# Decays moved into the mask tiles and onto the keys, GpSimd left out of the attention, and a new order of the loads

## The chip, the cores and the metric

One program on one core of a Trainium2 chip. The metric is the time of one execution in microseconds (us), median of three runs. The engines are named as in the profile: PE (TensorE; PEld is its weight load), DVE (VectorE), ACT (ScalarE), POOL (GpSimd) and SP, whose queue issues the DMAs.

## The reference

Retention attention (a causal product with a decay instead of a softmax), then two feed-forward blocks on the 2304 tokens of all batches:

```python
# q, k, v: (4 batches, 8 heads, 576 tokens, 64)
scores = scale * np.matmul(q, k.transpose(0, 1, 3, 2))
gamma = 1.0 - 2.0 ** (-5.0 - np.arange(H, dtype=np.float32))
Dmat = np.where(rel >= 0, gamma[:, None, None] ** rel[None, :, :], 0.0)   # rel = query position - key position
x = np.matmul(scores * Dmat[None, :, :, :], v)          # then to (2304, 512)
h = x @ w_in                                            # 512 -> 2048
x = (h * np.cos(h)) @ w_out
xn = x / rms * rms_g
g = xn @ w_gate                                         # 512 -> 1536
out = (silu(g) * (xn @ w_val)) @ w_out2
```

## The kernel before

The decay of a query at position i for a key at position j is gamma^i times gamma^-j. Tokens of a batch are cut into four chunks of 128 and one of 64 (`NFULL`, `REST`); a pair k is one chunk of two neighbouring batches, so there are ten pairs, 0 to 9: pairs 0 to 3 are the full chunks of batches 0 and 1, pair 4 their short one, 5 to 9 the same for batches 2 and 3.

For each chunk PE makes scores (`scores`, two PSUM banks), DVE multiplies them by the triangular mask (`masked`, two instructions), and PE multiplies the values by them (`values`). What earlier chunks add comes through a running sum of key times value (`sums_kv`), which ACT copies out of PSUM (`copy_state`) and PE multiplies by the queries (`from_state`). Before all this POOL has scaled the values by gamma^-j (`scale_values`), and behind it DVE scales the outputs by gamma^i while it takes them out of PSUM into `xall` (`result`, two instructions a pair); ACT makes the tables `gam` for that, one per chunk place (`decay`).

Weights of the first feed-forward block arrive as 64-bit words in 16 blocks w0 to w15 of 1 MiB. Each is turned into two float parts by eight steps in a chain: ACT size, DVE clamp, DVE shift, (ACT low), DVE high, DVE add, ACT cast, DVE rest. A step i of that block is a hidden product h_i (12 matmuls), the gate (ACT turns, DVE remainder, ACT sine, DVE product, ACT cast ghi, DVE low glo) and an output product out_i (12 matmuls). The first six steps (h0 to h5) take token tile 0 with w0 to w5, the next sixteen take token tile 1 with w0 to w15. Scores, masks and early hidden products share three PSUM banks (tag `g`), given out in turn.

The first 22 steps and the attention are laid out by a planner (`opening`, `lay_out`): each piece of work is a `Task` with an engine, an assumed duration and a key, and the order in which the planner picks them is the order of the instructions on each engine. The loads of the SP queue follow the list `PLAN`: a chunk's number, or -1 for the next weight block. Everything behind the opening is written out in a fixed order. The engines take their instructions strictly in that order.

Of the kernel before, what the change touches and what calls it, by code (L numbers as in the profile page):

```python
# [30 lines left out]
P = 128  # L31
# [9 lines left out]
NCH = NFULL + 1  # L41
NW1 = NF1
# [27 lines left out]
LEAD = 11.8  # L70
EARLY = 8
# [8 lines left out]
PLAN = [0, 5, 1, 6, 2, 7, -1, 3, 8, 4, 9, -1, 10, 15, 11, 16, -1, 12, 17, 13, 18, 14, 19, -1, -1, -1, -1, -1, -1, -1, -1, -1, -1, -1, -1, -1]  # L80
# [6 lines left out]
def body(ctx: ExitStack, tc, qkv, qkr, vr, w1, w2, rg, gq, gk, mask, out):  # L87
# [192 lines left out]
    first = []  # L280

    def load_tokens(part):
        for b, x in enumerate(first):
            nc.sync.dma_start(x[:, part], qkv[b, 0, :, part])

    def load(n):

        b, c = chunks[n]
        x = wa.tile([P, 4, DM], F32, tag="w", name="x")
        if n in (0, NCH):  # L290
            first.append(x)
            for src, dst in ((qkv[b, c, :, 0], x[:, 0]), (qkv[b, c, :, 1], x[:, 1]), (gk, gk_sb), (mask, mask_sb))[:2 if n else 4]:
                nc.sync.dma_start(dst, src)
        elif c < NFULL:
            nc.sync.dma_start(x, qkv[b, c])
        else:
            nc.sync.dma_start(x[:, :2, :NPAIR * REST], qkr[b])
            for a in range(2):
                nc.sync.dma_start(x[half(a), 2], vr[b])
        blocks = lambda a: a[:, :NPAIR * width(c)].rearrange("p (a i) -> p a i", a=NPAIR)  # L300
        ld[n] = blocks(x[:, 0]), blocks(x[:, 1]), x[:, 2], x[:, 3]
# [23 lines left out]
    def scores(n):  # L325
        w = width(chunks[n][1])
        kt, qt, _, _ = ld[n]
        ps = raw_scores[n] = [ps_tile().rearrange("p (h i) -> p h i", h=NPAIR) for _ in range(2)]
        for p in range(NPAIR):
            for hh in range(2):  # L330
                nc.tensor.matmul(ps[hh][keys(w, hh), p, :w], kt[half(hh), p, :], qt[half(hh), p, :], start=True, stop=True)

    def masked(n, hh):
# [4 lines left out]
                                mask_sb[r, r].unsqueeze(1).to_broadcast([w, NPAIR, w]), op=ALU.mult)  # L338

    def from_state(n):  # L340
        b, c = chunks[n]
        w, q, k = width(c), b % 2, b // 2 * NCH + c
        qt = ld[n][1]
# [22 lines left out]
    def copy_state(k):  # L366
        nc.scalar.copy(state, total[0])

    def values(n):
        b, c = chunks[n]  # L370
        w, q, k = width(c), b % 2, b // 2 * NCH + c
        vv = ld.pop(n)[2]
# [7 lines left out]
        del sc[n, 0], sc[n, 1]  # L380

    def result(k, a):
# [3 lines left out]
        nc.vector.tensor_tensor(x, outputs[k][a][..., :w], gam[c][:, a::2, :].unsqueeze(1).to_broadcast([P, 2, 2, w]), op=ALU.mult)  # L386
# [464 lines left out]
    def opening():  # L851

        lead = lambda k: 10.0 + 3.15 * k
        unit = lambda i: 31.3 + 6.8 * i if i < FIRST else 31.3 + 6.8 * FIRST + 20.0 * (i - FIRST)
# [3 lines left out]
        last_load = [None]  # L858

        def chain(x):  # L860
            last_load[0] = x
            return x

        for n in PLAN:
            if n >= 0:
                size = 0.0 if n == 0 else 1.5 if n == NCH else 2.45 if chunks[n][1] < NFULL else 0.95
                loads[n] = chain(Task("SP", size, lambda n=n: load(n), (), ones("wa"), behind=last_load[0]))
                if n == NCH:
                    parts = [chain(Task("SP", 1.25, lambda part=part: load_tokens(part), (), behind=last_load[0])) for part in (2, 3)]
                    gams = {0: chain(Task("SP", 0.6, lambda: nc.sync.dma_start(gam0, gq), (), behind=last_load[0]))}  # L870
            else:
                k = len(raws)
                raws[k] = chain(Task("SP", 2.45, lambda k=k: blocks1.append(Block(w1[k], wa if k < NSLOT_A else late["wb"])),
                                     (), ones("wa" if k < NSLOT_A else "wb"), behind=last_load[0]))
        for c in range(1, NCH):
            gams[c] = Task("ACT", 4 * 0.29, lambda c=c: decay(c), [gams[0]], key=lead(c) - 1.0)
        froms, before = {}, []
        for k in range(B // 2 * NCH):
# [5 lines left out]
            scaled = {n: Task("POOL", 1.25, lambda n=n: scale_values(n), [loads[n] if k else parts[0]], key=at) for n in pair}  # L884
# [440 lines left out]
```

## Time and profile before

| | |
|---|---|
| median of 3 runs | 890.64 us (889.91 to 890.96) |
| the profiled execution | 889.95 us |
| its span in the profile | 888.1 us (1.85 us lie around it) |
| busy share of the span | PE 97%, DVE 75%, ACT 52%, POOL 10% |
| mean granted clock of TensorE | 0.998 |

A row of the timeline gives start, duration, engine, line of the kernel, what is written from what, and in brackets how long the engine stood idle before it and what ended that. Durations of neighbouring instructions of one engine can overlap a little, so the distance from start to start is what one instruction costs.

### The profile page before, as it was taken

How to read it: one execution, taken by the hardware profiler on the slowest of the kernel's cores; microseconds unless marked ns; L12 is line 12 of the kernel's file. 1: busy time of each engine (PE TensorE's matmuls, PEld its weight loads, DVE VectorE, ACT ScalarE, POOL GpSimd, SP SyncE). 2: the span in 40 equal slices, each digit the busy share in tenths (PEclk: the TensorE clock that was granted, in tenths of full speed). 3: DMA queues.
4: the chain of work that ended last, by engine and by line, in shares of the span. 5: the costliest groups of instructions: out<-in, count | busy, mean ns of one | idle time of the engine just before them, and what ended most of it. 6: DMA issues, size and time to landing. Idle time of an engine off the chain costs nothing.

```text
span 888.1 us, 14679 instructions
## 1 busy us (share of the span) xinstructions
PE 862.8 (97%) x5738; PEld 785.9 (88%) x5738; DVE 666.3 (75%) x1004; ACT 464.2 (52%) x795; POOL 88.2 (10%) x97
## 2 busy tenths in 40 slices
PE   7797899999999999999999999999999999999998
PEld 6686688878888888998888999999999999999998
DVE  3897999947779977897874989698665598443594
ACT  3327687547565556675656755454443354333351
POOL 2340000000000000002343444100000000000000
PEclk9999999999999999999999999999999999999999
DMA  8999700124434443334786888998777798777793
GB/s 325 373 365 389 289 9 1 47 96 123 152 114 145 143 142 107 108 126 135 244 284 219 293 298 310 344 310 286 256 255 251 213 295 286 260 256 256 208 302 110
DMA packets 62085, 193.73 MB, mean 218 GB/s; under 512 B 5696, under 2 KB 23744, under 8 KB 53568
## 3 DMA queue, kind: packets, MB, share of 16 engines
q1 hardware_dynamic: 62016, 192.80, 63.7%
q8 instruction: 45, 0.74, 0.3%
q14 instruction: 24, 0.20, 0.1%
HBM read 143.49 MB, written 49.28 MB: 217 GB/s over the span
## 4 chain that ended last, share of the span: by engine, by line
PE 80%; DMA 8%; DVE 6%; ACT 2%; issue 2%; SPq 1%; POOL 1%; DVEq 0%; ACTq 0%; POOLq 0%
PE h L1077 14%; PE acc L1122 13%; PE acc L1077 13%; PE acc L242 9%; PE acc L241 9%; PE acc L243 9%; DMA raw<-w_dram 3%; PE h L242 3%; PE h L241 3%; PE h L243 3%; DMA x<-qkv_dram 3%; PE h L1122 2%; DVE w L135 2%; DMA so<-w 1%; POOL z L637 1%
## 5 line engine op out<-in xcount | busy, mean ns | idle before, releaser
L1077 PE MATMUL acc<-w 128*128 128x384 f32 x720 | 140.1, 335 | 0.5
L1077 PE MATMUL h<-w 128*128 128x384 f32 x720 | 139.0, 335 | 0.6 <-DVE SV L1059 0.6
L1077 PEld LDWEIGHTS acc<-w 128*128 128x128 f32 x720 | 125.5, 188 | 2.4 <-DVE v L1065 2.3
L1077 PEld LDWEIGHTS h<-w 128*128 128x128 f32 x720 | 125.8, 188 | 1.5 <-DVE SV L1059 1.2
L242 PE MATMUL acc<-glo,w 128*128 128x512 f32 (+1 forms) x320 | 118.0, 369 | 1.5 <-DVE glo L135 1.5
L241 PE MATMUL acc<-ghi,w 128*128 128x512 f32 (+1 forms) x320 | 118.4, 370 | 1.1 <-ACT ghi L513 1.1
L243 PE MATMUL acc<-ghi,w 128*128 128x512 f32 (+1 forms) x320 | 117.8, 368 | 0.0
L637 POOL TENSOR_TENSOR z<-z 128x256 f32<-128x256 f32 x72 | 64.6, 900 | 428.3 <-DMA z<-w 363.1
L1122 PE MATMUL acc<-w 128*128 128x256 f32 x846 | 104.1, 283 | 0.0
L1122 PEld LDWEIGHTS acc<-w 128*128 128x128 f32 x846 | 103.0, 191 | 0.2 <-DVE w L135 0.2
L241 PEld LDWEIGHTS acc<-ghi,w 128*128 128x128 f32 x320 | 60.3, 189 | 12.1 <-ACT ghi L513 1.5
L242 PEld LDWEIGHTS acc<-glo,w 128*128 128x128 f32 x320 | 60.3, 188 | 12.0 <-DVE glo L135 2.2
L243 PEld LDWEIGHTS acc<-ghi,w 128*128 128x128 f32 x320 | 60.4, 189 | 10.0
L1065 DVE TENSOR_TENSOR v<-s,acc 128x384 f32<-128x384 f32 x54 | 29.8, 551 | 52.3 <-PE acc L1077 39.5
L1105 ACT CAST w<-SV 128x768 fp32r<-128x768 f32 x55 | 42.5, 832 | 34.0 <-DVE SV L1110 18.2
L135 DVE TENSOR_TENSOR w<-SV,w 128x768 fp32r<-128x768 f32 x55 | 50.0, 953 | 13.5 <-ACT w L1105 13.5
L506 ACT ACTIVATE r<-r,half_pi 128x512 f32<-128x512 f32 (+1 forms) x80 | 54.6, 683 | 8.7 <-DVE r L503 8.5
L1043 ACT COPY s<-h 128x384 f32<-128x384 f32 x54 | 25.9, 480 | 58.9 <-PE h L1077 57.5
L241 PE MATMUL h<-xhi,w 128*128 128x512 f32 (+1 forms) x152 | 55.9, 368 | 0.0
L243 PE MATMUL h<-xhi,w 128*128 128x512 f32 (+1 forms) x152 | 55.8, 367 | 0.0
L241 PE MATMUL acc<-xhi,w 128*128 128x512 f32 (+1 forms) x152 | 55.8, 367 | 0.0
L243 PE MATMUL acc<-xhi,w 128*128 128x512 f32 (+1 forms) x152 | 55.7, 367 | 0.0
(126 smaller groups left out, 1568.1 us busy)
## 6 DMA issues: line engine op xcount, KB each, us to landing
w<-so SPq DMA_DIRECT2D x42, 768.0 KB, 6.1
w<-s SPq DMA_DIRECT2D x24, 1024.0 KB, 5.0
raw<-w_dram SPq DMA_DIRECT2D x36, 512.0 KB, 4.1
w<-s SPq DMA_DIRECT2D x24, 768.0 KB, 4.4
raw<-w_dram SPq DMA_DIRECT2D x16, 1024.0 KB, 10.8
x<-qkv_dram SPq DMA_DIRECT2D x14, 1024.0 KB, 14.5
s<-w SPq DMA_DIRECT2D x12, 1024.0 KB, 6.3
w<-t SPq DMA_DIRECT2D x36, 256.0 KB, 2.3
```

The lines of the kernel that those rows point to most:

```text
L135: eng.tensor_tensor(dst, src, hi.bitcast(F32), op=ALU.subtract)
L241: nc.tensor.matmul(dst, a[0], b[0], start=start, stop=False)
L242: nc.tensor.matmul(dst, a[0], b[1], start=False, stop=False)
L243: nc.tensor.matmul(dst, a[1], b[0], start=False, stop=stop)
L506: nc.scalar.activation(s["r"], s["r"], AF.Sin, bias=half_pi, scale=1.0)
L637: nc.gpsimd.tensor_tensor(z[:, dst], z[:, a], z[:, b], op=op)
L1043: nc.scalar.copy(t[:, :HALF], bank)
L1065: nc.vector.tensor_tensor(t, s, bank, op=ALU.add)
L1077: nc.tensor.matmul(bank, w[:, wp, kc * P:(kc + 1) * P], x[:, kc], start=k in (0, 1, 3) and kc == 0 and m == 0, stop=kc == 1 and m == 2, sk ...
L1105: nc.scalar.copy(t[:, 0], src)
L1122: nc.tensor.matmul(bank, s[:, a, i % 2, m * P:(m + 1) * P], wi[:, b], start=start and i == 0 and p == 0 and m % 2 == 0, stop=i == NPR - 1 ...
```

## The change

Values are no longer scaled and POOL does nothing in the attention. gamma^-j within a chunk goes into the mask: ACT makes three tables `falling` once, and `masked` multiplies by them. For the sums, ACT scales the keys in place by gamma^-j of the whole sequence, eight instructions for a pair (`scale_keys`), and puts the power of the chunk's place into the copy of the state, now four instructions (`copy_state`). `result` uses one table `gam` for all chunk places. A pair's operands lie in two tiles of 1 MiB (keys and queries of both chunks; values and keys by token of both chunks), the short pair's in one. `PLAN` now lists pairs: all of batches 0 and 1 come ahead of w0, pairs 5 to 7 ahead of w1, pair 8 ahead of w2, pair 9 ahead of w3.

```diff
-LEAD = 11.8
-EARLY = 8
+LEAD = 16.4
+EARLY = 7
...
-PLAN = [0, 5, 1, 6, 2, 7, -1, 3, 8, 4, 9, -1, 10, 15, 11, 16, -1, 12, 17, 13, 18, 14, 19, -1, -1, -1, -1, -1, -1, -1, -1, -1, -1, -1, -1, -1]
+PLAN = [0, 1, 2, 3, 4, -1, 5, 6, 7, -1, 8, -1, 9, -1, -1, -1, -1, -1, -1, -1, -1, -1, -1, -1, -1, -1]
...
-    def decay(c):
-        gam[c] = ap1.tile([P, NPAIR, width(c)], F32, name=f"gam{c}")
+    def fall(a):
+        r, w = (half(1), REST) if a == 2 else (slice(None), P)
         for p in range(NPAIR):
-            nc.scalar.activation(gam[c][:, p, :], gam0[:, p, :width(c)], AF.Copy, scale=later[:, c, p:p + 1])
...
-    def scale_values(n):
-        b, c = chunks[n]
-        v3 = ld[n][2].rearrange("p (h d) -> p h d", h=H)
-        nc.gpsimd.tensor_tensor(v3, v3, vg_sb[:, c, :].unsqueeze(2).to_broadcast([P, H, D]), op=ALU.mult)
+            nc.scalar.activation(falling[a][r, p, :], mask_sb[r, P - w:], AF.Copy, scale=factors[r, NCH + a, p:p + 1])
+
+    def scale_keys(k):
+        kk, c = ld[k][1][:, 2:], k % NCH
+        for h in range(H):
+            x = kk[:, :, h * D:(h + 1) * D]
+            nc.scalar.activation(x, x, AF.Copy, scale=decays[:, c * H + h:c * H + h + 1])
...
         nc.vector.tensor_tensor(s[r, :, :w], raw_scores[n][hh][r, :, :w],
-                                mask_sb[r, r].unsqueeze(1).to_broadcast([w, NPAIR, w]), op=ALU.mult)
+                                falling[hh if w == P else 2 * hh][r, :, :w], op=ALU.mult)
...
     def copy_state(k):
-        nc.scalar.copy(state, total[0])
+        for p in range(NPAIR):
+            nc.scalar.activation(state[:, :, p, :], total[0][:, :, p, :], AF.Copy, scale=factors[:, k % NCH + 1, p:p + 1])
...
-        nc.vector.tensor_tensor(x, outputs[k][a][..., :w], gam[c][:, a::2, :].unsqueeze(1).to_broadcast([P, 2, 2, w]), op=ALU.mult)
+        nc.vector.tensor_tensor(x, outputs[k][a][..., :w], gam[:, a::2, :w].unsqueeze(1).to_broadcast([P, 2, 2, w]), op=ALU.mult)
...
-        lead = lambda k: 10.0 + 3.15 * k
-        unit = lambda i: 31.3 + 6.8 * i if i < FIRST else 31.3 + 6.8 * FIRST + 20.0 * (i - FIRST)
+        lead = lambda k: 10.0 + 3.4 * k if k < 8 else 37.0 + 16.0 * (k - 8)
+        unit = lambda i: 39.0 + 12.3 * i if i < FIRST else 39.0 + 12.3 * FIRST + 5.4 * (i - FIRST)
...
+        for k in PLAN:
+            if k == 0:
+                start = [fetch(0.0, load_first, "wa"), fetch(1.3, lambda: load(0, 0, range(1, 2)))]
+                loads[0] = [start[1], fetch(2.5, lambda: load(0, 1), "wa")]
+                gams = fetch(0.7, lambda: nc.sync.dma_start(gam, gq))
+            elif k > 0:
+                loads[k] = [fetch(2.5, lambda k=k, side=side: load(k, side), "wa") for side in range(1 if k % NCH == NFULL else 2)]
...
-            scaled = {n: Task("POOL", 1.25, lambda n=n: scale_values(n), [loads[n] if k else parts[0]], key=at) for n in pair}
...
+                adding = [Task("ACT", 8 * 0.29, lambda k=k: scale_keys(k), [loads[k][1]], key=at - 1.0)]
                 for n in pair:
-                    sums = [Task("PE", 0.52, lambda n=n: sums_kv(n), [scaled[n], loads[n] if k else parts[1]] + before + sums, ones("st") if c == 0 and n == pair[0] else (),
-                                 key=at + 0.1, more=0.25, mode="columns")]
-                before = [Task("ACT", 0.55, lambda k=k: copy_state(k), sums + last + froms.get(k - 1, []), (),
+                    adding = [Task("PE", 0.52, lambda n=n: sums_kv(n), before + adding, ones("st") if c == 0 and n == pair[0] else (),
+                                   key=at + 0.1, more=0.25, mode="columns")]
+                before = [Task("ACT", 4 * 0.3, lambda k=k: copy_state(k), adding + last + froms.get(k - 1, []), (),
```

What this does to the order, at three places. First SP, from the table `gam` on, before: 1 MiB of one chunk a row, w0 behind the chunks of pairs 0 to 2.

```order
L870 DMA gam_93<-gq_dram 128x512
L295 DMA x<-qkv_dram 128x2048 x4
L167 DMA raw<-w_dram 128x2048
L295 DMA x<-qkv_dram 128x2048 x2
L297 DMA x<-qkr_dram 128x2x256
L299 DMA x<-vr_dram 64x512 x2
```

The same place of the change:

```order
L882 DMA gam<-gq_dram 128x512
L296 DMA x<-xy_dram 128x2048 x6
L293 DMA x<-xr_dram 128x2048
L168 DMA raw<-w_dram 128x2048
L296 DMA x<-xy_dram 128x2048 x6
L168 DMA raw<-w_dram 128x2048
```

Three loads of 1 MiB (the second half of six, and the short pair) have moved ahead of w0.

Second DVE, from the clamp of w0 (L147) on, before; s are masked scores, t is the block in work.

```order
L147 TENSOR_SCALAR t<-t 128x1024
L337 TENSOR_TENSOR s_425<-g,mask_sb 128x512
L337 TENSOR_TENSOR s_427<-g,mask_sb 128x512
L150 TENSOR_SCALAR t<-t 128x1024
L337 TENSOR_TENSOR s_449<-g,mask_sb 128x512
L337 TENSOR_TENSOR s_459<-g,mask_sb 128x512
L156 SCALAR_TENSOR_TENSOR t<-raw,t 128x1024
L159 ISA t<-raw,t 128x2048
L386 TENSOR_TENSOR xall<-po,gam_258 128x2x2x128 x2
```

The change, from the second chunk of pair 2 on to the clamp of w0 (L148) and what follows it:

```order
L348 TENSOR_TENSOR s_431<-g,falling_93 128x512
L348 TENSOR_TENSOR s_441<-g,falling_94 128x512
L400 TENSOR_TENSOR xall<-po,gam 128x2x2x128 x2
L348 TENSOR_TENSOR s_511<-g,falling_93 128x512
L348 TENSOR_TENSOR s_523<-g,falling_94 128x512
L148 TENSOR_SCALAR t<-t 128x1024
L348 TENSOR_TENSOR s_547<-g,falling_93 128x512
L348 TENSOR_TENSOR s_549<-g,falling_94 128x512
```

The results of pair 2 (the row into xall) and the masks of pair 3's first chunk now stand ahead of the clamp of w0; before, the clamp, shift, high and add of w0 stood ahead of those results.

Third ACT, before, from the size of w5 to the cast of h1: L500 is the turns of h1, L506 its sine, the second L143 the size of w6.

```order
L143 ACTIVATE t<-raw 128x1024
L500 ACTIVATE r<-g,quarter 128x512
L153 ACTIVATE raw<-raw 128x1024
L143 ACTIVATE t<-raw 128x1024
L506 ACTIVATE r<-r,half_pi 128x512
L153 ACTIVATE raw<-raw 128x1024
L513 CAST ghi<-r 128x512
```

The change, from the size of w5 on, with the same steps at L144, L514, L520, L154 and L527 (the first L527 is the cast of h0):

```order
L144 ACTIVATE t<-raw 128x1024
L527 CAST ghi<-r 128x512
L514 ACTIVATE r<-g,quarter 128x512
L379 ACTIVATE state<-total,gk_sb 128x2x64 x4
L520 ACTIVATE r<-r,half_pi 128x512
L154 ACTIVATE raw<-raw 128x1024
L144 ACTIVATE t<-raw 128x1024
L527 CAST ghi<-r 128x512
```

The sine of h1 now stands ahead of the size of w6 and behind a copy of the state.

Behind the opening the instructions of each engine stand in the same order in both kernels.

## Rows read from the trace of the kernel before

**Rows 1.** The page: span, and busy time of each engine.
```profile
span 888.1 us, 14679 instructions
PE 862.8 (97%) x5738; PEld 785.9 (88%) x5738; DVE 666.3 (75%) x1004; ACT 464.2 (52%) x795; POOL 88.2 (10%) x97
```

**Rows 2.** Stretches: length, busy PE, PEld, DVE, ACT, POOL; clock, DMA share, GB/s.
```profile
60.00:81.00 21.00, 19.70 (x272) 16.22 (x268) 17.71 (x23) 10.60 (x13) 4.13 (x4) 1.00 0.95 348
81.00:109.00 28.00, 23.02 (x184) 17.75 (x180) 25.89 (x36) 20.15 (x26) 0.00 (x0) 1.00 0.79 314
115.00:190.00 75.00, 75.00 (x332) 62.10 (x332) 68.62 (x87) 50.03 (x68) 0.00 (x0) 1.00 0.04 15
```

**Rows 3.** Timeline of PE: first matmuls of h1, h3 and out4.
```profile
69.81 0.50 PE L241 MATMUL g<-xhi,w 128*128 128x512 f32 x1 [1.30 <-DVE r L509]
...
93.38 0.50 PE L241 MATMUL g<-xhi,w 128*128 128x512 f32 x1 [1.40 <-DVE r L509]
...
109.64 0.50 PE L241 MATMUL acc<-ghi,w 128*128 128x512 f32 x1 [1.05 <-ACT ghi L513]
```

**Rows 4.** Timeline of DVE, from pair 2's results to the add of w5.
```profile
33.79 1.28 DVE L386 TENSOR_TENSOR xall<-po,gam 128x512 f32<-128x512 f32 x2
34.99 1.27 DVE L337 TENSOR_TENSOR s<-g,mask_sb 128x512 f32<-128x512 f32 x2
...
39.05 0.69 DVE L147 TENSOR_SCALAR t<-t 128x1024 f32<-128x1024 f32 x1 [0.57 <-ACT t L143]
...
82.53 0.69 DVE L509 TENSOR_TENSOR r<-g,r 128x512 f32<-128x512 f32 x1 [3.65 <-ACT r L506]
...
84.07 0.69 DVE L135 TENSOR_TENSOR glo<-r,ghi 128x512 fp32r<-128x512 f32 x1 [0.25 <-ACT ghi L513]
...
91.51 1.22 DVE L135 TENSOR_TENSOR w<-t,w 128x1024 fp32r<-128x1024 f32 x1
92.64 0.68 DVE L509 TENSOR_TENSOR r<-g,r 128x512 f32<-128x512 f32 x1
93.24 0.68 DVE L147 TENSOR_SCALAR t<-t 128x1024 f32<-128x1024 f32 x1
93.84 0.87 DVE L337 TENSOR_TENSOR s<-g,mask_sb 64x256 f32<-64x256 f32 x2
...
95.35 0.69 DVE L150 TENSOR_SCALAR t<-t 128x1024 int32<-128x1024 int32 x1
96.07 1.23 DVE L156 SCALAR_TENSOR_TENSOR t<-raw,t 128x1024 int32<-128x1024 int32 x1
97.33 1.22 DVE L159 CUSTOM_DVE_ANT_0 t<-raw,t 128x2048 uint16<-128x2048 uint16 x1
```

**Rows 5.** Timeline of DVE: first, longest and last instruction beside POOL after 33.8 us.
```profile
36.18 1.50 DVE L135 TENSOR_TENSOR w<-t,w 128x1024 fp32r<-128x1024 f32 x1
...
40.51 2.00 DVE L156 SCALAR_TENSOR_TENSOR t<-raw,t 128x1024 int32<-128x1024 int32 x1
...
64.98 1.84 DVE L159 CUSTOM_DVE_ANT_0 t<-raw,t 128x2048 uint16<-128x2048 uint16 x1
```

**Rows 6.** Timeline of POOL: values of chunk 1, and those beside the 40.51 us row.
```profile
15.18 1.04 POOL L313 TENSOR_TENSOR x<-x,gk_sb 128x512 f32<-128x512 f32 x1 [4.55 <-DMA x<-qkv_dram]
...
40.38 1.04 POOL L313 TENSOR_TENSOR x<-x,gk_sb 128x512 f32<-128x512 f32 x1 [3.78 <-DMA x<-qkv_dram]
```

**Rows 7.** Timeline of ACT: decay tables, turns, sizes of w0 and w6, sine of h1.
```profile
12.63 2.45 ACT L306 ACTIVATE gam<-gam,gk_sb 128x128 f32<-128x128 f32 x8 [10.40 <-DMA gam<-gq_dram]
...
25.41 1.14 ACT L143 ACTIVATE t<-raw 128x1024 f32<-128x1024 f32 x1 [3.71 <-DMA raw<-w_dram]
...
76.35 0.67 ACT L500 ACTIVATE r<-g,quarter 128x512 int32<-128x512 f32 x1
...
80.76 1.13 ACT L143 ACTIVATE t<-raw 128x1024 f32<-128x1024 f32 x1 [2.68 <-DMA raw<-w_dram]
81.79 0.70 ACT L506 ACTIVATE r<-r,half_pi 128x512 f32<-128x512 f32 x1
```

More of the change, by code (lines that the diff above doesn't have):

```diff
@@ L278, in half @@
         return slice(a * D, (a + 1) * D)
[L280 to L286, printed above, removed]
-        b, c = chunks[n]
[L289 to L295, printed above, removed]
-        else:
[L297 to L301, printed above, removed]
@@ L857, in opening, with fetch @@
         ones = lambda *names: {name: 1 for name in names}
[L858 to L870, printed above, removed]
-            else:
[L872 to L876, printed above, removed]
+        queue = []
+        def fetch(size, run, *take):
+            queue.append(Task("SP", size, run, (), ones(*take), behind=queue[-1] if queue else None))
+            return queue[-1]
+        for k in PLAN:
[5 more added lines that the diff above has]
+                loads[k] = [fetch(2.5, lambda k=k, side=side: load(k, side), "wa") for side in range(1 if k % NCH == NFULL else 2)]
+            else:
+                i = len(raws)
+                raws[i] = fetch(2.5, lambda i=i: blocks1.append(Block(w1[i], wa if i < NSLOT_A else late["wb"])), "wa" if i < NSLOT_A else "wb")
+        falls = [Task("ACT", 1.17 if a < 2 else 0.95, lambda a=a: fall(a), [start[0]], key=lead(0) - 5.0 if a < 2 else lead(3)) for a in range(3)]
         froms, before = {}, []
@@ L883, in opening @@
             bank = "acc" if k < EARLY else "g"
-            scaled = {n: Task("POOL", 1.25, lambda n=n: scale_values(n), [loads[n] if k else parts[0]], key=at) for n in pair}
             masks = {}
             for n in pair:
-                score = Task("PE", 0.89 if full else 0.45, lambda n=n: scores(n), [loads[n]], {"g": 2}, key=at - 2.0, more=0.25, mode="rows")
-                masks[n] = [Task("DVE", 0.6 if full else 0.35, lambda n=n, hh=hh: masked(n, hh), [score], ones(f"s{hh}"), ones("g"), key=at - 2.0)
-                            for hh in range(2)]
+                score = Task("PE", 0.89 if full else 0.45, lambda n=n: scores(n), [start[0] if n == 0 else loads[k][0]], {"g": 2},
+                             key=at - 2.0, more=0.25, mode="rows")
+                masks[n] = [Task("DVE", 0.6 if full else 0.35, lambda n=n, hh=hh: masked(n, hh), [score, falls[hh if full else 2 * hh]],
+                                 ones(f"s{hh}"), ones("g"), key=at - 2.0) for hh in range(2)]
             held = {bank: 1 if k < EARLY else 2}
@@ L894, in opening @@
                     last = [Task("PE", 0.45 if full else 0.22, lambda n=n: from_state(n), masks[n] + before + last, held if n == pair[0] else (),
-                                 key=at, more=0.25, mode="quarters")]
+                                 ones("wa") if full and n == pair[1] else (), key=at, more=0.25, mode="quarters")]
                 froms[k] = last
+            adding = []
             if full:
-                sums = last
+                adding = [Task("ACT", 8 * 0.29, lambda k=k: scale_keys(k), [loads[k][1]], key=at - 1.0)]
@@ L903, in opening @@
+                before = [Task("ACT", 4 * 0.3, lambda k=k: copy_state(k), adding + last + froms.get(k - 1, []), (),
                                ones("st") if c == NFULL - 1 else (), key=at - 1.0)]
-                last = sums
             for n in pair:
-                last = [Task("PE", 0.79 if full else 0.42, lambda n=n: values(n), masks[n] + last + [scaled[n]],
-                             held if c == 0 and n == pair[0] else (), {"s0": 1, "s1": 1, "wa": 1}, key=at + 0.2, more=0.25, mode="columns")]
+                after = masks[n] + last + loads[k] + (adding if n == pair[1] else [])
@@ L908, in opening @@
+                give = {"s0": 1, "s1": 1, "wa": 0 if n == pair[0] else 2 if c == 0 else 1}
+                last = [Task("PE", 0.79 if full else 0.42, lambda n=n: values(n), after, held if c == 0 and n == pair[0] else (), give,
+                             key=at + 0.2, more=0.25, mode="columns")]
             freed = [{}, {bank: 1}] if k < EARLY else [{bank: 1}] * 2
-            done = [Task("DVE", 0.6 if full else 0.35, lambda k=k, a=a: result(k, a), last + [gams[c]], (), freed[a], key=at - 0.5) for a in range(2)]
+            done = [Task("DVE", 0.6 if full else 0.35, lambda k=k, a=a: result(k, a), last + [gams], (), freed[a], key=at - 0.5) for a in range(2)]
```

82 lines of the change are left out of this document (59 added, 23 removed).

## The prediction, made before the result was known

> **What bounds the kernel now.** I read the page first: PE is busy for 97% of the span [rows 1]. Then the stretches: from 115 to 190 us PE is busy for all of the 75 us, while between 60 and 109 us it idles for 1.3 and 5.0 us [rows 2]. PE's work is the same in both kernels and everything behind the opening keeps its order, so the change can only move the moment at which the opening's idle time is over. That moment is out4: ahead of it PE waits once more, 1.05 us up to 109.64 us [rows 3], and from 115 us on for nothing in 75 us [rows 2]. Whatever out4 gains or loses should go through to the end unchanged.
>
> Next I asked who sets PE's pace before that. h1 and h3 start when DVE has made the product of the hidden step before them [rows 3]. They take a PSUM bank in turn, and the product frees it. For h3 the product stands at 92.64 to 93.3 us in DVE's row [rows 4], and PE starts h3 at 93.38. From there to the wait at 108.6 us PE works without a gap: 15 us. So DVE's queue up to the product of h2 is the path. Its waits after 33.8 us are six, the first 0.57 and the last 0.25 us, 5.9 us together; one of them is 3.65 us long and ends with ACT's sine [rows 4]. That sine stood behind the size of w6 in ACT's queue, which waited for w6 to land [rows 7]. DVE is nearly full, and its instructions are lengthened where POOL works beside it [rows 5, 6].
>
> **The change, part by part.** I take DVE from 33.79 us, where pair 2's results begin, to 93.3 us, the end of h2's product, and correct it term by term.
>
> *Loads: w0 comes later.* Three loads of 1 MiB move ahead of w0. The pace: chunk 1 lands at 15.18 us [rows 6], and w0, four loads of 1 MiB later, at 25.41 us [rows 7]: 2.56 us for 1 MiB. At chunk 1 some 3.34 MiB have been issued (two chunks, three tables, chunk 1); the change needs 10.34 MiB up to w0 (tables, pairs 0 to 4, w0), 7.0 more, so w0 lands near 15.2 + 17.9 = 33.1 us. Its size takes 1.1 us [rows 7], and the clamp can start at 34.2 us. Ahead of that clamp DVE's row holds only attention (pairs 0 to 2 and a chunk of pair 3), so it must wait there. At 34.2 us it has done pair 2's results (1.20 us from start to start [rows 4]), which the kernel before had not; but the clamp, shift, high and add of w0 that it had done are still to come: 0.60 + 0.72 + 1.26 + 1.26 = 3.84 us at the distances of rows 4 (I take the add like the high). Net 2.64 us, and 0.4 us because 34.2 is later than 33.8: **+3.0 us**.
>
> *Order at the end.* In the change the rest of w4 (1.13 us) comes behind the product of h2 and the masks of pair 9's second chunk (0.9 us) come ahead of it: **-0.2 us** [rows 4].
>
> *POOL leaves.* Six of DVE's instructions after 33.8 us are longer than the same ones without POOL beside them. The first is the rest of w0, 1.50 us, the longest the high of w1, 2.00 us, the last the add of w2, 1.84 us [rows 5]; alone they take 1.22, 1.23 and 1.22 us [rows 4]. The six extras run from 0.28 to 0.83 us and sum to 3.5 us: **-3.5 us**. Masks and results read PSUM; two of them take 1.27 and 1.28 us in the middle of that stretch [rows 4], no more than elsewhere, so I give them nothing.
> The high of w1 shows the size of it: POOL's instruction stands at 40.38 to 41.42 us [rows 6], DVE's starts at 40.51 and is 0.77 us longer than alone [rows 4, 5]. [...] If each of the six meetings had cost a whole POOL instruction of 1.04 us, the term would be 6.2 us and the time 2.7 us lower; the rows say 3.5, and the measured extras are what I sum.
>
> *Waits that go.* In the change the sine of h1 stands ahead of the size of w6 in ACT's row, and w3 to w6 are loaded right behind pair 9 without a piece of attention between: the 3.65 us wait has no cause left. In the tally all 5.9 us come off: **-5.9 us**, and the waits of the change are put in anew.
>
> *Waits that come.* (a) Between the product of h0 and the remainder of h1 DVE's row now has only a shift and a low, 0.72 + 0.6 us. But h1 needs the bank that this product frees, then its 12 matmuls (15 us for h3, out2, h4, h5, out3 and short attention gives 2.8 us each) and the turns on ACT, 0.67 us [rows 7]: 3.8 us with the hand-overs, so DVE waits about **+2.5 us**. Queued behind it are the high and add of w3, so all later blocks. (b) Small waits of the kind that remain before, 2.3 us (5.9 less 3.65) [rows 4]; with POOL's hand-over gone from the sums and fewer loads to wait for I take half: **+1.1 us**. Lower bound for both together: nothing, if another bank is free. Upper bound: 5.9 us, as before.
>
> *ACT's new work.* A table of 128 columns costs 2.45/8 = 0.31 us [rows 7]. Keys: 8 x 0.31 = 2.45 us for each of eight full pairs; state: 4 x 0.31 = 1.2 us, by the nearest row, since no row has it from PSUM at 128 columns (lower bound 0.67 us for 512 columns in one piece, upper bound twice the 1.2). Together some 3.7 us a full pair, while the pair's two loads alone take 5.1 us at the pace above. The cover is ACT's idle time, 10.4 of 21 us from 60 to 81 us [rows 2]. Cost nothing on the path; where the cover fails is the third rival. The masks read a full table in place of a repeated one. Results, which read such a table already, take 1.28 us for two and masks 1.27 us [rows 4]: nothing, at most 0.2 us for all 40.
>
> *Sum.* 93.3 + 3.0 - 0.2 - 3.5 - 5.9 + 2.5 + 1.1 = 90.3 us for the end of h2's product, 3.0 us earlier. Behind it PE has the same 15 us up to out4, with one new wait of about 0.3 us for the rest of w5. Out4's own wait of 1.05 us [rows 3] was for the cast of h4's gate. In the change nothing but a low, a shift and a high stands between h4's steps on DVE while PE works at out2, h5 and out3, so I let it shrink to nothing: 3.0 - 0.3 + 1.1 = 3.8. Pair 0, whose sums no longer wait for POOL, adds nothing, since DVE waits at w0 anyway. I forecast **4 us** less: 889.95 - 4 = 885.95 for an execution like the profiled one. The median stands 0.7 us above that execution, so 886.6 us for the median.
>
> **Rivals.** *First: no net gain.* Scores and masks pass the same three banks, with DVE and PE now both without slack from 34 us on. If this costs 0.4 us at each of the seven pairs still to come, waits are 2.8 us above mine, and out4 gains about 1 us: 889.6 us for the median. For it: before, PE waited for masks at several scores in this stretch. Against: DVE's small waits there sum to only 2.3 us.
>
> *Second: more gain.* DVE waits for nothing from 34.2 us on. Then the new waits of 3.6 us fall away as well: 7.4 us less, 883.2 us. For it: 25.89 of 28 us were busy from 81 to 109 us even with the 3.65 us wait in it [rows 2]. Against: the bank loop of h1, which the order shows.
>
> *Third, slower: loads set the pace through ACT's queue.* The size of w2 stands ahead of the copy of pair 7's state and of the cast of w1, and the keys of pair 8 ahead of it. w2 is 17.0 MiB behind chunk 1: at 2.56 us for 1 MiB it lands at 58.7 us, its size ends at 59.8, and DVE's clamp of w2, by the tally, is due near 61 us. At the 348 GB/s of the stretch from 60 to 81 us [rows 2] 1 MiB takes 3.0 us; then w2 lands at 66.2 us, the clamp starts at 67.3, 6.3 us late, and out4 comes 2.5 us later than before: 893.1 us. The sign turns from about 2.9 us for 1 MiB on. For it: that row, and small pieces no longer explain it if it stays. Against: before, the slow stretches held the short chunks' many small pieces, and the change loads rows of 8 KB instead.
>
> **How the numbers follow.** The forecast (between 2 and 7 us less) has 0.54, the first rival 0.20, the second 0.08, the third 0.18. About 0.2%, 1.8 us, is what a measurement of this kernel can tell from no change: 888.8 to 892.4 us count as the same. The forecast and the second rival are faster, 0.62; the first is the same, with a little of the third, 0.21; the rest slower, 0.17. The range reaches from 882 us, a bit below the second rival, to 892 us, which takes in the first and falls short of the third.
>
> **What would show it.** In the trace of the changed kernel: w0 landing near 33 us and DVE's clamp of it at about 34; the highs, adds and rests at 1.2 us everywhere; no wait of 3 us or more on DVE between 40 and 95 us, but one of 2 to 3 us ahead of the remainder of h1; h3 near 90.4 us; out4 near 105 us without a wait ahead of it. Wrong would be: ACT waiting for a raw block with casts behind it, PE waiting for masks in every pair, or a later stretch giving the lead back.

## The result, and the profile after

| | before | after |
|---|---|---|
| median of 4 runs each, side by side | 890.8 us | 878.03 us (877.3 to 878.36) |
| ratio, 95% interval | 1 | 0.9857 [0.984, 0.9875] |
| the profiled execution, its span | 889.95 us, 888.1 us | 878.32 us, 876.4 us |

The change takes 12.7 us off (1.43% of 890.6), three times the 4 us of the forecast and below the range. The page of the changed kernel, span and busy time:

```profile
span 876.4 us, 14711 instructions
...
PE 861.5 (98%) x5738; PEld 785.0 (90%) x5738; DVE 659.9 (75%) x1004; ACT 486.2 (55%) x879; POOL 65.3 (7%) x77
```

Against [rows 1], PE has 1.3 us less and DVE 6.4 us less to do; ACT has 22 us more. Timeline of PE, changed kernel: the first matmuls of h1, h3 and out4, and the longest later wait.

```profile
67.57 0.47 PE L242 MATMUL g<-xhi,w 128*128 128x512 f32 x1 [1.33 <-DVE s L348]
...
85.12 0.50 PE L242 MATMUL g<-xhi,w 128*128 128x512 f32 x1 [0.45 <-DVE r L523]
...
99.19 0.39 PE L242 MATMUL acc<-ghi,w 128*128 128x512 f32 x1
...
185.11 0.51 PE L242 MATMUL h<-xhi,w 128*128 128x512 f32 x1 [0.75 <-DMA xhi<-kept_x]
```

Against [rows 3], h3 starts 8.26 us earlier (its wait is 0.45 us, where it was 1.40), and out4 starts 10.45 us earlier, without a wait. So almost all of the 11.7 us of span is won before out4. Timeline of DVE, changed kernel: clamp of w0, rest of w0, product of h0, remainder of h1, product of h2.

```profile
33.19 0.69 DVE L148 TENSOR_SCALAR t<-t 128x1024 f32<-128x1024 f32 x1 [1.69 <-ACT t L144]
...
42.61 1.22 DVE L136 TENSOR_TENSOR w<-t,w 128x1024 fp32r<-128x1024 f32 x1
...
69.67 0.69 DVE L523 TENSOR_TENSOR r<-g,r 128x512 f32<-128x512 f32 x1
...
71.66 0.68 DVE L517 SCALAR_TENSOR_TENSOR r<-r,g 128x512 f32<-128x512 int32 x1
...
84.38 0.69 DVE L523 TENSOR_TENSOR r<-g,r 128x512 f32<-128x512 f32 x1
```

Where [rows 4] have waits of 0.25 to 3.65 us, DVE now shows no wait behind the clamp of w0 until 95 us, and the rest of w0 takes 1.22 us (1.50 in [rows 5]). Timeline of ACT, changed kernel: keys and state of pair 0, sizes of w0 and w6.

```profile
10.33 2.44 ACT L324 ACTIVATE x<-x,gk_sb 128x128 f32<-128x128 f32 x8 [3.61 <-DMA x<-xy_dram]
13.78 1.14 ACT L379 ACTIVATE state<-total,gk_sb 128x128 f32<-128x128 f32 x4 [1.00 <-PE total L374]
...
32.00 1.16 ACT L144 ACTIVATE t<-raw 128x1024 f32<-128x1024 f32 x1 [1.52 <-DMA raw<-w_dram]
...
74.14 1.16 ACT L144 ACTIVATE t<-raw 128x1024 f32<-128x1024 f32 x1
```

In [rows 7] the size of w6 waited 2.68 us for its load; now it starts 6.6 us earlier and waits for no load. What has changed with the loads is plain in the stretches (columns as in [rows 2]; the last two of a row are DMA share and GB/s). Before:

```profile
25.00:30.00 5.00, 3.35 (x70) 2.73 (x69) 3.59 (x6) 2.17 (x2) 1.04 (x1) 1.00 1.01 366
30.00:35.00 5.00, 4.40 (x96) 3.97 (x92) 4.85 (x7) 1.55 (x2) 2.64 (x2) 1.00 1.06 271
55.00:60.00 5.00, 5.00 (x104) 4.54 (x105) 5.00 (x7) 0.59 (x1) 2.54 (x2) 1.00 1.02 368
60.00:65.00 5.00, 5.00 (x72) 3.93 (x70) 4.83 (x8) 0.69 (x1) 2.34 (x3) 1.00 0.87 268
```

After:

```profile
30.00:35.00 5.00, 3.58 (x87) 3.07 (x84) 3.31 (x6) 2.67 (x4) 0.00 (x0) 1.00 1.01 410
60.00:65.00 5.00, 5.00 (x64) 4.12 (x60) 4.86 (x8) 4.00 (x5) 0.00 (x0) 1.00 1.02 419
60.00:81.00 21.00, 19.67 (x214) 15.69 (x211) 20.58 (x29) 17.68 (x24) 0.00 (x0) 1.00 1.01 413
81.00:109.00 28.00, 27.51 (x180) 22.22 (x179) 27.34 (x37) 21.54 (x31) 0.00 (x0) 1.00 0.59 238
```

Before, the loads drop to 268 to 368 GB/s in two stretches of 10 us; these are the ones in which the small pieces of the short chunks are under way. At 271 GB/s the DMA engines were no less busy (share 1.06) than at 410 (1.01), so there the transfers themselves are slow. From 60 to 65 us the share is 0.87, so part of that dip is DMA engines without work: the load of w3 was issued only at 63.08 us. After, there is no dip, 60 to 81 us run at 413 GB/s in place of 348 [rows 2], and PE's idle time from 81 to 109 us shrinks from 4.98 to 0.49 us.

### The profile page after: what moved, and what is told of

It reads as the page before. It is cut to its first block, busy times and chain, and to the rows that moved or that the text cites. A ratio compares the mean times of both kernels' runs of the same rounds, so it can differ in the third digit from the quotient of the medians.

```text
span 876.4 us, 14711 instructions
## 1 busy us (share of the span) xinstructions
PE 861.5 (98%) x5738; PEld 785.0 (90%) x5738; DVE 659.9 (75%) x1004; ACT 486.2 (55%) x879; POOL 65.3 (7%) x77
## 4 chain that ended last, share of the span: by engine, by line
PE 87%; DVE 6%; DMA 4%; ACT 2%; issue 1%; POOL 0%; SPq 0%; DVEq 0%; ACTq 0%; POOLq 0%
PE h L1091 14%; PE acc L1091 13%; PE acc L1136 13%; PE acc L243 11%; PE acc L244 11%; PE acc L242 11%; PE h L242 4%; PE h L243 4%; PE h L244 3%; DMA raw<-w_dram 2%; PE h L1136 2%; DVE w L136 1%; DVE s L348 1%; DMA gam<-gq_dram 1%; DMA xhi<-kept_x 1%
## 5 line engine op out<-in xcount | busy, mean ns | idle before, releaser
L1119 ACT CAST w<-SV 128x768 fp32r<-128x768 f32 x55 | 42.5, 832 | 34.2 <-DVE SV L1124 18.3
L520 ACT ACTIVATE r<-r,half_pi 128x512 f32<-128x512 f32 (+1 forms) x80 | 54.7, 684 | 8.1 <-DVE r L517 7.8
L242 PE MATMUL h<-xhi,w 128*128 128x512 f32 (+1 forms) x152 | 56.0, 369 | 1.0 <-DMA xhi<-kept_x 1.0
L527 ACT CAST ghi<-r 128x512 fp32r<-128x512 f32 (+1 forms) x80 | 46.1, 577 | 17.5 <-DVE r L523 17.1
```

Of the source, the lines that this page charges most:

```text
L242: nc.tensor.matmul(dst, a[0], b[0], start=start, stop=False)
L520: nc.scalar.activation(s["r"], s["r"], AF.Sin, bias=half_pi, scale=1.0)
L527: nc.scalar.copy(s["hi"], s["r"])
L1119: nc.scalar.copy(t[:, 0], src)
```

## The experiments

Theory A is the prediction's: DVE's queue is the path, shortened by POOL's leaving and by single waits. Theory C: the loads are a second path close under it. "Gain" is (1 - ratio) x 890.6 us, each ratio taken against the kernel before on the same chip; the intervals reach 1.2 to 2.5 us to either side.

| run | us | ratio [interval] | gain | h3 starts |
|---|---|---|---|---|
| order alone | 891.92 | 1.0018 [1.0003, 1.0033] | -1.6 | 94.04 |
| no scaling on POOL | 889.22 | 0.9981 [0.9968, 0.9994] | 1.7 | 93.32 |
| sine first | 889.09 | 0.9984 [0.9972, 0.9996] | 1.4 | 93.15 |
| short chunk in one transfer | 886.37 | 0.9943 [0.9927, 0.996] | 5.1 | 89.82 |
| the same, no scaling | 885.09 | 0.993 [0.9915, 0.9945] | 6.2 | 89.79 |
| the same, sine first | 884.63 | 0.993 [0.9908, 0.9952] | 6.2 | 88.13 |
| all three | 884.12 | 0.9924 [0.9896, 0.9951] | 6.8 | 88.87 |
| two-tile operands alone | 882.02 | 0.9903 [0.9883, 0.9924] | 8.6 | 86.10 |
| the same, no scaling | 876.64 | 0.984 [0.9823, 0.9858] | 14.2 | 81.76 |
| two-tile operands and decays | 880.95 | 0.9891 [0.9874, 0.9909] | 9.7 | 85.79 |
| **the change** | 878.03 | 0.9857 [0.984, 0.9875] | 12.7 | 85.12 |
| change, short pair in pieces | 881.96 | 0.9892 [0.9877, 0.9907] | 9.6 | 88.67 |
| change, POOL beside | 879.25 | 0.9867 [0.9851, 0.9882] | 11.8 | 86.07 |
| change, keys not scaled | 878.84 | 0.987 [0.9856, 0.9885] | 11.6 | 85.69 |

**One part alone.** The order of the change on the kernel before (its `PLAN` unfolded into chunks, its `lead`, `unit`, `LEAD`, `EARLY`):

```diff
-LEAD = 11.8
-EARLY = 8
+LEAD = 16.4
+EARLY = 7
-PLAN = [0, 5, 1, 6, 2, 7, -1, 3, 8, ...
+PLAN = [0, 5, 1, 6, 2, 7, 3, 8, 4, 9, -1, 10, 15, ...
```

> The kernel before with the change's order of loads and its planner keys, but POOL still scaling the values. Theory A (DVE's queue is the path; POOL beside it costs some 4 us, DVE's waits 6 us): the waits go, POOL's part stays, 5 to 8 us under the kernel before, some 884 us. Theory B (the order alone does it, POOL and the decays are worth nothing): all 12.7 us, 878 us.

No gain at all. ACT in that run waits for the blocks w0 and w1 (sizes):

```profile
36.62 1.17 ACT L143 ACTIVATE t<-raw 128x1024 f32<-128x1024 f32 x1 [6.51 <-DMA raw<-w_dram]
...
54.09 1.16 ACT L143 ACTIVATE t<-raw 128x1024 f32<-128x1024 f32 x1 [6.00 <-DMA raw<-w_dram]
```

The operands and decays without the order:

```diff
-LEAD = 16.4
-EARLY = 7
+LEAD = 11.8
+EARLY = 8
-PLAN = [0, 1, 2, 3, 4, -1, 5, 6, 7, -1, 8, -1, 9, ...
+PLAN = [0, 1, 2, -1, 3, 4, -1, 5, 6, -1, 7, 8, 9, ...
```

> The change with pairs and weight blocks loaded about as before (w0 behind pair 2, w1 behind pair 4, w2 behind pair 6) and the planner keys of before. Theory A: POOL's 4 us are gained, waits stay, 885 to 888 us. Theory B: 890 to 891 us as before, or more for ACT's new work.

9.7 us: theory A puts the gain into the wrong part. On top of these operands the order brings the other 2.9 us (880.95 to 878.03); without them, nothing.

POOL's scaling left out of the kernel before:

```diff
-        nc.gpsimd.tensor_tensor(v3, v3, vg_sb[:, c, :]...to_broadcast([P, H, D]), op=ALU.mult)
+        pass
```

> The kernel before without the scaling of the values on POOL (the values go in unscaled, so the decay of the keys is left out); every other instruction in the same order. Theory A: DVE's highs, adds and rests take 1.2 us everywhere, 3.5 to 4.6 us come off its queue, time 886 to 887.5 us. Theory B: 890.5 us, no change.

The size of w6 moved behind the sine of h1 (`sized` keeps the size tasks, a2 is the sine):

```diff
+            if i == 1:
+                sized[6].after.append(a2)
```

> The kernel before with one move on ACT: the size of w6 (and its low step) behind the sine of h1. Theory A: DVE's 3.65 us wait shrinks to under 1 us and the end comes 2.5 to 3.7 us earlier, 887 to 888 us. Theory B: no change, 890.5 us, because something else ends last at h3.

The terms of 3.5 and 3.65 us are worth 1.7 and 1.4 us alone, and h3 moves by 0.06 and 0.23 us. Without POOL's scaling DVE's instructions are short, but it waits the time away; its remainder of h1 in that run:

```profile
82.47 0.69 DVE L509 TENSOR_TENSOR r<-g,r 128x512 f32<-128x512 f32 x1 [3.43 <-ACT r L506]
```

The sine still stands behind w6, and w6 lands when it lands. With the sine first, the size of w6 still waits 1.35 us for its load; now the cast of h1's gate stands behind it, and DVE waits 1.66 us for that cast. This is where theory C comes from.

**The transfers.** In the kernel before, a short chunk in one transfer of 128x1024 (keys, queries and the values twice, laid side by side in memory), nothing else changed on any engine:

```diff
-            nc.sync.dma_start(x[:, :2, :NPAIR * REST], qkr[b])
-            for a in range(2):
-                nc.sync.dma_start(x[half(a), 2], vr[b])
+            flat = x.rearrange("p s m -> p (s m)")
+            nc.sync.dma_start(flat[:, :2 * DM], xr[b])
...
```

> The kernel before with one edit: the keys, queries and values of a chunk of 64 tokens come in one transfer of 128x1024 (rows of 4 KB) in place of three (128x2x256, rows of 1 KB, and two of 64x512, rows of 2 KB); bytes, order on every engine and all else as before. Theory A (VectorE's queue alone is the path; loads are hidden): within 1 us of before, 890 to 891.5. Theory C (loads are a second path just under VectorE's; before loses some 5 us of load time in the stretches with these pieces: 366 and 271 GB/s at 25 to 35 us, 368 and 268 at 55 to 65, against 415 to 419 around them): those stretches at 400 GB/s or more, w6 lands 4 to 6 us earlier, the 3.65 us wait for the sine of h1 shrinks or goes, and 886 to 889.

And in the changed kernel the reverse, the short pair in six pieces (two with rows of 1 KB, four with rows of 2 KB):

```diff
-                nc.sync.dma_start(x.rearrange("p s m -> p (s m)"), xr[r])
+                for q in range(2):
+                    nc.sync.dma_start(x[:, :2, q * NPAIR * REST:(q + 1) * NPAIR * REST], ...
+                    for a in range(2):
+                        nc.sync.dma_start(x[half(a), 2 + q], xr[r][half(a), (2 + q) * DM:(3 + q) * DM])
...
```

> The changed kernel with one edit: the operands of a pair of short chunks come in six transfers (two of 128x2x256, rows of 1 KB, and four of 64x512, rows of 2 KB), as the kernel before has them, in place of one of 128x2048; bytes and order on every engine as in the changed kernel. Theory A: 878 plus or minus 0.8. Theory C: two dips to about 270 to 370 GB/s, some 4 to 5 us of load time lost by 60 us, w0 2 us or more later than 32.0 us, and 880.5 to 883.5.

Both as theory C has it: 5.1 us won by the one, 3.1 us lost by the other (12.7 to 9.6). Two stretches of the kernel before with one transfer:

```profile
30.00:35.00 5.00, 5.00 (x108) 4.50 (x105) 4.21 (x4) 0.59 (x1) 3.83 (x4) 1.00 1.03 424
60.00:65.00 5.00, 5.00 (x78) 4.01 (x78) 4.86 (x7) 1.12 (x2) 2.88 (x3) 1.00 1.02 417
```

Its first matmul of h3:

```profile
89.82 0.50 PE L241 MATMUL g<-xhi,w 128*128 128x512 f32 x1 [1.40 <-DVE r L511]
```

The changed kernel with the pieces:

```profile
25.00:30.00 5.00, 4.64 (x96) 4.03 (x96) 2.11 (x4) 2.53 (x9) 0.00 (x0) 1.00 1.09 301
60.00:65.00 5.00, 4.84 (x108) 4.47 (x107) 4.96 (x7) 3.91 (x7) 0.00 (x0) 1.00 1.04 323
```

The dips go and come with the pieces alone. No run separates their short rows (1 and 2 KB) from the 64 partitions that the pieces of values go into, but the single packets kept in the trace of the kernel before speak for the second. From 28 to 29 us, when hardly any but the 1 KB rows (into all partitions) ran beside the long ones, such a row took 46 ns, one of 8 KB 313 ns, and the loads came at 395 GB/s. From 29 to 33 us, with the 64x512 pieces under way, the same rows took 60 to 87 and 516 to 562 ns, at 225 to 255 GB/s (medians, us by us). Rows of 2 KB took 137 to 146 ns in those pieces, but 84 ns in the transfers of all 128 partitions (kept_x) from 74 to 77 us. This points to pieces into 64 partitions that slow the other loads beside them; a run with such pieces alone was not made.

**Cures together.** One transfer and no scaling:

> The same edit, and GpSimd's scaling of the values left out as in the run without scaling (the values go into the sums unscaled). Alone, leaving out the scaling brought 1.3 us. Theory A: the single transfer adds nothing, 889 to 890. Theory C: what VectorE gains without GpSimd is no longer taken back by waits for loads, so the two add to more than the sum of both alone: 882 to 885, and the product of h2 ends 3 us or more before 93 us.

One transfer and the sine first:

> The kernel before with two edits: one transfer for a short chunk, and the size of w6 behind the sine of h1; GpSimd scales as before. Theory C: with loads and the sine's place cured, only GpSimd beside VectorE is left, so the run against the one with all three edits is the price of GpSimd where it is on the path: 884 to 885.5, so 1 to 3 us above that one. Rival: 886.4, as with the single transfer alone.

All three:

> The kernel before with three edits at once: one transfer for a short chunk, GpSimd's scaling left out (values go into the sums unscaled), and ScalarE's size of w6 moved behind the sine of h1. Alone they brought 4.9, 1.3 and 1.4 us; the first two together 6.1 with the product of h2 where the first alone has it, and a wait of 3.06 us for the sine. Theory C (each covers for the others: loads, GpSimd beside VectorE, and the sine in ScalarE's queue end within some 3 us of each other): the wait for the sine goes, the product of h2 ends at 86 to 87.5 (93.3 before), and 882 to 884.5. Rival (what is left of the gain is in the decays and the order alone): as with two edits, 885 to 886.

The times are 885.09, 884.63 and 884.12 us: the first just misses its range, the other two lie in theirs, but what was to stand behind them did not come. One transfer and no scaling were to bring more than the 6.8 us of both alone, and bring 6.2. With all three, h2's product was to end at 86 to 87.5 us and h3 starts at 88.87; and POOL's scaling, which was to cost 1 to 3 us between the last two runs, is not seen there (0.5 us, within the intervals). In the first, h3 stands where the single transfer alone has it, since size w6 still waits for its load (2.35 us) and the sine behind it (3.06 us). With all three, size w6 still waits 1.50 us for its load, and DVE 1.65 us for the cast of h1's gate behind it. Small pieces, POOL and the sine were not all.

**Layout against decays.** The two-tile operands with everything else as before (masks, POOL's scaling, planner's keys); the diff is against the run with two-tile operands and decays:

```diff
-            nc.scalar.activation(x, x, AF.Copy, scale=decays[...])
...
+        nc.gpsimd.tensor_tensor(v3, v3, vg_sb[:, c, :]...to_broadcast([P, H, D]), op=ALU.mult)
...
-                                falling[hh if w == P else 2 * hh][r, :, :w], op=ALU.mult)
+                                mask_sb[r, r].unsqueeze(1).to_broadcast([w, NPAIR, w]), op=ALU.mult)
```

> The kernel before with the operands of a pair in two tiles (and the pair of short chunks in one transfer of 128x2048), the pairs loaded in the order 0, 1, 2, w0, 3, 4, w1, 5, 6, w2, 7, 8, 9; GpSimd scales the values, masks, gam tiles and the planner's keys are those of before. With the decays moved as well this gave 880.95. Theory C (the transfers bring most): 882.5 to 885.5, loads at 400 GB/s or more throughout, and what is left to the run with the decays is GpSimd beside VectorE. Rival (the decays bring most): 886 or more.

And without the scaling:

> The run before this one with GpSimd's scaling left out (values go into the sums unscaled). Theory C: where loads no longer bind, GpSimd's leaving is worth 1.5 to 3.5 us (1.3 in the kernel before, 3.5 by the prediction), so 880 to 883, and ScalarE's scaling of the keys in the changed kernel costs nothing against it. Rival (GpSimd's price is hidden again): within 0.8 us of the run before it.

This gives the two prices. The layout alone brings 8.6 us, 3.5 more than the one transfer: its opening runs at 264 GB/s in the first 10 us (213 before), and pairs and blocks come in another order; these two were not separated. POOL's leaving, worth 1.7 us before, is worth 5.4 us (882.02 to 876.64) where loads keep ahead, more than the 1.5 to 3.5 us expected. DVE beside POOL in the layout alone, two of seven such instructions:

```profile
30.66 1.79 DVE L160 CUSTOM_DVE_ANT_0 t<-raw,t 128x2048 uint16<-128x2048 uint16 x1
...
59.95 1.95 DVE L157 SCALAR_TENSOR_TENSOR t<-raw,t 128x1024 int32<-128x1024 int32 x1
```

The extras over 1.22 us for one (1.28 for two rests of x) sum to 5.2 us, and h3 comes 4.34 us earlier without POOL. What one meeting costs can be read from both engines' starts. In the kernel before, the high of w1 began 0.91 us before POOL's product ended [rows 5, 6] and took 0.77 us longer; the rest of w0 began 0.42 us before the end of the product below and took 0.28 us longer. In all 18 meetings with an extra from 30 us on, in the two kernels with POOL's scaling and in the next run, it is what was left of POOL's product, less 0.14 us. POOL's product was lengthened too where it came second: DVE's high of w2 began first, and the product beside it took 2.00 us in place of 1.04. POOL and DVE, kernel before:

```profile
35.56 1.04 POOL L313 TENSOR_TENSOR x<-x,gk_sb 128x512 f32<-128x512 f32 x1 [0.79 <-DMA x<-vr_dram]
...
63.63 1.21 DVE L156 SCALAR_TENSOR_TENSOR t<-raw,t 128x1024 int32<-128x1024 int32 x1
...
63.75 2.00 POOL L313 TENSOR_TENSOR x<-x,gk_sb 128x512 f32<-128x512 f32 x1 [0.48 <-DMA x<-vr_dram]
```

POOL put back beside the changed kernel, writing a tile that nobody reads, points the same way:

```diff
+            for n in pair:
+                Task("POOL", 1.25, lambda n=n: beside(n), loads[k], key=at)
```

> The changed kernel with twenty products of 128x512 on GpSimd that read values and decays and write a tile that nothing reads, one for each chunk of a batch as soon as its operands have landed; nobody waits for them, and the order on the other engines is that of the changed kernel. It prices GpSimd beside VectorE where loads wait for nobody. Theory A (the term of 3.5 us that the prediction gave to GpSimd leaving, in full): 881 to 882. Theory C (VectorE is the path behind w0's landing, so only the products that run behind it count, with 0.3 to 0.8 us on each VectorE instruction beside them): 879 to 881.

Three meetings, extras of 0.11, 0.36 and 0.77 us, 1.24 in sum; h3 is 0.95 us later and the time 0.9 (by the ratios) to 1.2 us (by the medians) longer, which by itself is within the intervals. So the sum of the extras comes near the price, where DVE is the path.

The decays in the changed kernel, priced on ACT (the keys go unscaled into the sums):

```diff
-            nc.scalar.activation(x, x, AF.Copy, scale=decays[:, c * H + h:c * H + h + 1])
+        pass
```

> The changed kernel without ScalarE's scaling of the keys (64 products of 128x2x64, some 19.5 us of ScalarE's queue; the sums are made with unscaled keys); the order on all engines is that of the changed kernel. The prediction gave this work nothing, since ScalarE has idle time. If that holds: 877.3 to 878.8. Rival (ScalarE's queue holds back casts, turns and states that VectorE and TensorE wait for, which would be why the decays gave back 4.3 of the 5.4 us that GpSimd's leaving was worth on the two-tile operands): 874 to 876.5.

19.5 us of ACT's work taken away bring nothing: h3 comes at 85.69 us (85.12 in the change). The granted clock was 0.66 from 35 to 40 us in the profiled execution, so a gain of some tenths could be hidden; one of 2 us or more hardly (an estimate: 0.34 of those 5 us is 1.7 us of PE's time).

**The banks.** The three banks under names of their own, taken in turn:

```diff
-            return psa.tile([P, 512], F32, tag="g", bufs=3, name="g")
+            turns[0] += 1
+            return psa.tile([P, 512], F32, tag=f"g{turns[0] % 3}", bufs=1, name="g")
```

> The changed kernel with the three banks of scores and first products given out in strict turn, which is what the prediction took them to be; the order on the engines is the changed kernel's. The prediction's term: the product of h1 waits for the bank that the product of h0 frees (about 70.4 us, 67.57 in the changed kernel), VectorE waits 2 to 3 us before the remainder of h1, and 880 to 881. Rival (the bank is not what h1 waits for, or the delay is taken up by VectorE's other work): 878 plus or minus 0.8.

884.52 us, 0.9929 [0.99, 0.9957], 6.4 us slower than the change and above the 880 to 881 expected. In that run PE starts h1 and DVE comes to its remainder so:

```profile
70.82 0.79 PE L244 MATMUL g<-xhi,w 128*128 128x512 f32 x1 [4.14 <-DVE r L525]
...
71.83 0.63 PE L246 MATMUL g<-xhi,w 128*128 128x512 f32 x1
...
77.06 0.69 DVE L519 SCALAR_TENSOR_TENSOR r<-r,g 128x512 f32<-128x512 int32 x1 [4.92 <-ACT r L516]
```

The stretch around h1 (the third number from the end is the granted clock):

```profile
70.00:80.00 10.00, 9.18 (x79) 7.13 (x80) 4.61 (x8) 4.74 (x9) 0.00 (x0) 0.66 1.02 424
```

The wait that the prediction foresaw is there, and longer: after 4.14 us of idling the granted clock is 0.66 from 70 to 80 us (0.50 from 70 to 75), most of h1's matmuls take 0.63 us where those ahead of the wait take 0.39 to 0.40, and the 6.4 us hold the price of the clock too.

**Versions that might have been better.** w0 loaded ahead of pairs 3 and 4:

```diff
-PLAN = [0, 1, 2, 3, 4, -1, 5, 6, 7, ...
+PLAN = [0, 1, 2, -1, 3, 4, 5, 6, 7, ...
```

> The changed kernel with the load of w0 moved ahead of the operands of the pairs 3 and 4 (one number of the load order moves; the order written out for the engines follows from it). VectorE's waits of 2.88 and 1.69 us ahead of 33.2 us could then be filled with w0's conversion. If VectorE's queue alone bounds the changed kernel: 874 to 876.5. If loads are the second path there as well, pairs 3 and 4 land 2.5 us later and their masks wait: 877.5 to 880.

880.45 us, 0.9883 [0.9851, 0.9915]. The four rests of x on POOL:

```diff
-                xs_of[s].append(Task("DVE", 0.6, lambda t=t, kc=kc: rest_x(t, kc), ...
+                xs_of[s].append(Task("DVE" if s else "POOL", 0.6 if s else 1.3, ...
```

> The changed kernel with the four rests of x for the first token tile (0.68 us each in VectorE's queue at 45 to 50 us) on GpSimd, which has nothing else to do there. If VectorE's queue alone sets the end of the opening in the changed kernel: 2.4 to 2.7 us less in it, and 875 to 876.5. If GpSimd beside VectorE takes it back (some 0.8 us for each operation at worst): 877.5 to 879.

879.61 us, 0.9875 [0.9854, 0.9896]: DVE lost 2.6 us of work and h2's product came at 84.89 us, not earlier; the planner's order changed with it, and DVE waited elsewhere. Keys scaled on POOL, in the order of the change and in that of before:

```diff
-                adding = [Task("ACT", 8 * 0.29, lambda k=k: scale_keys(k), ...
+                    scaled = Task("POOL", 1.25, lambda k=k, q=q: scale_keys(k, q), ...
```

> The changed kernel with the keys scaled on GpSimd, sixteen products of 128x512, in place of ScalarE's 64; masks and states as in the changed kernel; the order written out follows from it. If ScalarE's scaling is what costs: 875.5 to 878, since GpSimd beside VectorE cost 1.2 us for twenty products in the changed kernel. If GpSimd beside VectorE costs what it did on the two-tile operands alone (5.4 us): 880 to 883.

> The run with the decays and the two-tile operands in the order of before (880.95), with the keys scaled on GpSimd in place of ScalarE. If GpSimd's place in the order is what makes it dear: 881 to 883, as with the layout alone (882.0). If ScalarE's scaling is dearer: 878 to 880.5.

879.93 and 880.66 us, 0.9882 [0.9868, 0.9897] and 0.9886 [0.9868, 0.9903]. None of these versions, which leave nothing out, beats the change.

## Why the prediction was wrong

**The steps that failed** are two. The larger part of the number hangs on wait (a): "But h1 needs the bank that this product frees". That step put in 2.5 us where the changed kernel shows none: h1 started at 67.57 us, 2.8 us before h0's product ended at 70.36. The three banks are not given out in turn here, though the description of the kernel says that they are. With wait (b) this makes 3.6 of the 7.7 us that were missed.

The other failed in the mechanism: "So DVE's queue up to the product of h2 is the path." The loads were a second path just under it. POOL's scaling left out moved h3 by 0.06 us, the new layout by 7.28, both together by 11.62. The dips were seen: the third rival says that "the slow stretches held the short chunks' many small pieces", but only as an argument against a loss. No term of the sum took them as a gain. With one transfer of 128x2048 instead, the loads ran at 410 GB/s or more from 10 to 65 us. The -3.5 and -5.9 us of the sum came off all the same, since the new layout kept the loads ahead. That they came in full is in part luck: on the layout of before, no scaling and the sine first bring 1.7 and 1.4 us, and the order alone nothing.

**The account of the miss.** By the profiles the span lost 11.7 us where 4.0 were forecast. Of the other 7.7 us, 5.2 stand at the end of h2's product (85.1 us, forecast 90.3): the waits (a) and (b), 3.6 us, did not come; w0's clamp came at 33.2 us in place of 34.2; 0.6 is spread. Then pair 9's products from the state and of the first values, 1.2 us on PE, stand ahead of h3 in the changed kernel and stood behind it before: I counted the same 15 us to out4. The 0.3 us wait for the rest of w5 did not come either, and a wait near 465 us (476 before) fell from 1.27 to 0.27 us. This makes 7.7.

**Term by term.** *w0 later, +3.0:* it landed at 32.0 us, 1.1 us sooner than worked out, since the opening's loads ran at 261 GB/s in the first 10 us (213 before) and then at 410 to 424. *Order at the end, -0.2:* not contradicted. *POOL leaves, -3.5:* the method, summing the extras, holds; what it is worth depends on the loads: 1.7 us before, 5.4 on the new layout. The 6.2 us set against it took a whole POOL product of 1.04 us in each meeting; the rows show what was left of it, less 0.14 us. *Waits that go, -5.9:* they went, but the largest of them was a load's, and curing ACT's order alone was worth 1.4 us. *Wait (a), +2.5:* false. What h1 waited for was a mask (1.33 us on PE), and DVE's row has no wait there. With the banks forced into turn, DVE's wait is 4.9 us. *Wait (b), +1.1:* none is shown. *ACT's new work, nothing:* right, also for the state from PSUM, 1.14 us for four (1.2 estimated).

**The rivals.** The second, more gain, had the right direction and mechanism on DVE, but not its cause, and stopped at 883.2 us. The third named the loads and looked only at what would be lost by them.

**Open.** The decays with the layout in the order of before (880.95 us) are 4.3 us slower than the layout without scaling (876.64, which leaves out work). In the order of the change ACT's keys cost nothing, and keys on POOL in the old order give 880.66; how much of the 4.3 us is the planner's order and how much waits that ACT causes there was not separated. Nor was the price of ACT's keys tried in the old order. Before, the granted clock was 0.92 and 0.74 in the two stretches from 40 to 50 us, and in the changed kernel 1.00 in both; no run separates what that was worth. DVE's only wait for PE there was 0.62 us, which bounds it as far as DVE's queue is the path.

## What to carry to other kernels

Where two paths end within a few us of each other, the gain of each cure alone is small and their sum is no estimate for all together (here no scaling on POOL was worth 1.7 us alone and 5.4 on the new layout): work out when the second path would let the wait end, before giving a term its full price. A stretch in which DMA engines are fully busy at two thirds of the rate (here 271 GB/s at a share of 1.06, against 410 at 1.01) is time lost on every load behind it; ask which transfers stand in it, and count a change of their shape as a term of its own. A wait worked out from a rotation of buffers must be read from how they are handed out in a trace, not from their number (here 2.5 us were put in and none shown).

## What the runs showed of the hardware

- Pieces of 128x2x256 and 64x512 (rows of 1 and 2 KB) took the loads from 406 to 424 GB/s down to 268 to 368 in 5 us stretches, with the DMA engines' share at 1.01 to 1.09 (0.87 in one). The packets speak for the pieces into 64 partitions as the cause: beside them 8 KB rows of other loads took 516 to 562 ns from 29 to 33 us in the kernel before, where the median was 313 from 28 to 29.
- POOL's product of 1.04 us lengthened a DVE instruction beside it by 0.11 to 0.84 us: by what was left of the product when DVE's instruction began, less 0.14 us. A product that came second itself took 2.00 us (kernel before, at 63.75 us).
- With the banks in turn, a PE wait of 4.14 us was followed by matmuls of 0.63 to 0.79 us, where those ahead of it took 0.39 to 0.40, at a granted clock of 0.66 from 70 to 80 us.
- An ACT product of 128x2x64 took 0.31 us from SBUF (2.44 for 8) and 0.285 from PSUM (1.14 for 4).
